# Half blocks with their two parts stacked, one more group of x copied out of PSUM, and three low halves of the weights made by GpSimd

## The chip, the cores and the metric

The kernel runs on one core of a Trainium2 chip. The metric is the device time of one execution in microseconds. Before the change it is 1144.92 us, the median of three runs (1144.85 to 1145.62).

## What is computed

Attention over channels, and behind it a layer of eight experts of which each token takes one:

```python
qn = q / (norm(q, axis=1) + 1e-6);  kn = k / (norm(k, axis=1) + 1e-6)   # B=4, N=5056, C=256
s = kn.transpose(0, 2, 1) @ qn / tau                                    # 256 x 256 a batch
a = softmax(s, -1)
x = (v @ a).reshape(20224, 256)
logits = x @ w_gate                                                     # 8 experts
e = argmax(logits);  gate_w = softmax(logits)[e]
out = gate_w * (relu(x @ w1[e]) @ w2[e])                                # w1 256 x 1024, w2 1024 x 256
```

## The kernel before

**Two float16 parts for each number.** A float32 number is held as a high and a low float16 part, and a product is three matmuls: high by high, high by low, low by high. The weights are sixteen half matrices (w1 and w2 of eight experts, 128 x 4096 float16 each with both parts, in the tile W). For each, `w_high` (ScalarE, L147) writes the high parts and `w_low` (VectorE, L151) the low ones, from float32 data that were loaded into the place of a neighbouring half matrix. So the halves are made in two chains, one from each end: the odd half of a pair may be written only when the low part of the even half has been read out, and the next pair begins behind that. In `lay`'s names they are ("high", i, k) and ("low", i, k), with even i in one chain and odd i in the other.

**The opening, up to about 140 us.** SyncE loads batch 0 of q and k (raw), the weights (W, wraw), batch 1 of q and k, and v. TensorE multiplies what has come: the products q·k (px, then sp, L187), a sum of squares of each weight half for its scale (gram, L128), and x of batch 0. x goes by groups g of 512 tokens in T = 4 tiles of 128 (`product`, L1205, 4 banks of PSUM, the tile px4; one more column by `bound`, L1210). The first AHEAD = 8 groups are read where they stand in px4: VectorE chooses the experts (`chosen`, L392 to L402) and a scale (`scaled`, L93), ScalarE writes the rows' high parts (L368), VectorE the low ones (L372), `rank` on TensorE (L421, L424) and `slots` give each token its place, and GpSimd scatters the four tiles' rows to DRAM (L460, DMA_INDIRECT). Groups 8 and 9 of batch 0 and all of batches 1 to 3 go by another way: one tile in a PSUM buffer of the pool ps_a, copied out by ScalarE (`copied`, L1299), and then worked on from SBUF (xg, two buffers). The pseudo task "handed" closes px4 and opens the PSUM pools of the expert blocks; the first block's first product waits for all reads of px4.

**The blocks.** A block is a run of sorted tokens of one expert: 72 blocks of 256 tokens while the batches come in, then 13 of 128 and 5 of 64 (half blocks). It needs eight pieces of weights, 128 x 1024 float16 each, copied from W to wp by VectorE (L734) or ScalarE (L741), because the expert's number is known only on the chip. `first` (L752) makes h = w1·x, with 12 matmuls a piece; `relu` (ScalarE, L760) and `rest` (VectorE, L763) write h's two parts to ht; `second` (L776) makes y with the token tile as weights (128 x 128, and 128 x 64 in a half block) and 256 columns of w2, six matmuls a piece and tile of tokens; `result` (ScalarE, L790) scales y and `store` (GpSimd, L794) scatters it to the output.

**What sets the order.** The programs of TensorE, ScalarE, VectorE and SyncE are written out by `lay`, a list planner: each `task` has an engine, a cost in us, the tasks it needs, a due time, and rings of buffers. Costs and due times decide only the order; on the chip each engine runs its own list in order and waits for semaphores. Pieces may go to ScalarE if it is free earlier. GpSimd's transfers are spaced by the planner's `RUN` and `REST`.

## Time and profile before

| | |
|---|---|
| median of three runs | 1144.92 us |
| the profiled execution | 1141.65 us, of which 1139.6 us are the span |
| TensorE (PE) busy | 1123.1 us, 99% of the span |
| VectorE (DVE) | 883.9 us, 78% |
| ScalarE (ACT) | 751.7 us, 66% |
| GpSimd (POOL) | 352.2 us, 31% |
| chain that ended last | TensorE 86%, DMA 7%, issue 3%, VectorE 2% |

A row of the timeline gives the start in us, the length, the engine, the line, the operation and its tiles, the number of equal instructions in the row, and, in brackets, for how long the engine stood idle and what ended that. TensorE's matmuls overlap: the distance from one row's start to the next row's start is what the row costs, and its length is longer than that.

### The profile page before, as it was taken

How to read it: one execution, taken by the hardware profiler on the slowest of the kernel's cores; microseconds unless marked ns; L12 is line 12 of the kernel's file. 1: busy time of each engine (PE TensorE's matmuls, PEld its weight loads, DVE VectorE, ACT ScalarE, POOL GpSimd, SP SyncE). 2: the span in 40 equal slices, each digit the busy share in tenths (PEclk: the TensorE clock that was granted, in tenths of full speed). 3: DMA queues.
4: the chain of work that ended last, by engine and by line, in shares of the span. 5: the costliest groups of instructions: out<-in, count | busy, mean ns of one | idle time of the engine just before them, and what ended most of it. 6: DMA issues, size and time to landing. Idle time of an engine off the chain costs nothing.

```text
span 1139.6 us, 28806 instructions
## 1 busy us (share of the span) xinstructions
PE 1123.1 (99%) x10325; PEld 985.8 (87%) x10325; DVE 883.9 (78%) x2562; ACT 751.7 (66%) x1558; POOL 352.2 (31%) x335
## 2 busy tenths in 40 slices
PE   9889999999999999999999999999999999999997
PEld 8778788988888878888888877888888888888897
DVE  6798686888888867778788876778777777867886
ACT  5565587698887877679897787477766555332232
POOL 0035442245334401243434411224343323232121
PEclk9999999999999999999999999999999999999999
DMA  9999688267764665265765575333332223222221
GB/s 367 408 406 354 168 266 261 71 183 211 198 205 115 168 186 143 76 176 146 202 205 146 127 211 171 75 93 96 104 103 66 75 57 73 57 76 53 46 43 40
DMA packets 155859, 177.42 MB, mean 156 GB/s; under 512 B 116866, under 2 KB 117124, under 8 KB 155712
## 3 DMA queue, kind: packets, MB, share of 16 engines
q1 hardware_dynamic: 139968, 132.74, 42.0%
q0 software_dynamic: 15744, 42.79, 11.1%
q8 instruction: 83, 1.36, 0.5%
q14 instruction: 64, 0.52, 0.1%
HBM read 111.48 MB, written 42.97 MB: 136 GB/s over the span
## 4 chain that ended last, share of the span: by engine, by line
PE 86%; DMA 7%; issue 3%; DVE 2%; POOL 1%; ACT 0%; SPq 0%; POOLq 0%; ACTq 0%
PE y L776 35%; PE hp L752 34%; PE px L1293 7%; DMA raw<-in_qk 4%; PE sp L209 3%; DMA W<-in_w 3%; PE sp L187 2%; PE px L1205 2%; PE sp L210 2%; POOL out L794 1%; DMA v<-in_vT 1%; PE px L1286 1%; PE px L187 0%; DVE ht L763 0%; DVE rows L372 0%
## 5 line engine op out<-in xcount | busy, mean ns | idle before, releaser
L776 PE MATMUL y<-wp,ht 128*128 128x256 f16 (+1 forms) x3888 | 482.2, 273 | 0.0
L752 PE MATMUL hp<-xT,wp 128*128 128x256 f16 (+2 forms) x4320 | 476.7, 260 | 0.5 <-DVE wp L734 0.5
L752 PEld LDWEIGHTS <-wp 128*128 128x128 f16 x4320 | 383.0, 98 | 46.7 <-DVE wp L734 3.2
L776 PEld LDWEIGHTS <-ht 128*128 128x128 f16 (+1 forms) x3888 | 376.1, 98 | 45.6 <-DVE ht L763 0.2
L734 DVE COPY wp<-W 128x1024 f16 x637 | 274.4, 443 | 112.5 <-PE hp L752 84.5
L760 ACT ACTIVATE ht<-hp 128x512 f16<-128x512 f32 (+1 forms) x324 | 189.7, 587 | 198.3 <-PE hp L752 180.9
L794 POOL DMA_INDIRECT out<-o,mt x162 | 168.2, 1038 | 480.2 <-ACT o L790 365.0
L460 POOL DMA_INDIRECT xs<-rows,r_si x160 | 178.5, 1116 | 294.9 <-ACT W L147 70.5
L763 DVE SCALAR_TENSOR_TENSOR ht<-hp,ht 128x512 f16<-128x512 f32 (+1 forms) x324 | 219.1, 677 | 33.9 <-ACT ht L760 32.1
L790 ACT ACTIVATE o<-y,b_fac 128x256 f32<-128x256 f32 (+1 forms) x162 | 69.2, 468 | 53.4 <-PE y L776 35.0
L1293 PE MATMUL px<-a_h,hl 128*128 128x264 f16 x480 | 99.4, 276 | 0.0
L741 ACT COPY wp<-W 128x1024 f16 x83 | 85.6, 1040 | 3.5 <-PE y L776 2.6
L1293 PEld LDWEIGHTS <-hl 128*128 128x128 f16 x720 | 68.5, 98 | 9.5
L179 DVE SCALAR_TENSOR_TENSOR hl<-raw,qk_s,hl 128x512 f16<-128x512 f32 x80 | 56.5, 747 | 23.0 <-ACT hl L172 23.0
L172 ACT ACTIVATE hl<-raw,qk_s 128x512 f16<-128x512 f32 x80 | 53.3, 713 | 21.8 <-PE sp L210 20.7
L1293 PE MATMUL px<-a_l,hl 128*128 128x264 f16 x240 | 66.2, 276 | 0.0
L1425 ACT ACTIVATE nraw<-nraw 128x1024 f32<-128x1024 f32 x60 | 63.1, 1052 | 2.1 <-DMA nraw<-in_qkc 2.1
L1299 ACT COPY xg<-px 128x264 f32<-128x264 f32 x128 | 47.4, 371 | 24.7 <-PE px L1293 19.1
L368 ACT ACTIVATE rows<-xg,x_sc 128x256 f16<-128x256 f32 x128 | 55.9, 500 | 9.2 <-DVE x_sc L93 8.8
L1305 ACT ACTIVATE xjunk<-xg 128x256 bf16<-128x256 f32 x128 | 53.1, 415 | 2.8
L372 DVE SCALAR_TENSOR_TENSOR rows<-xg,x_sc,rows 128x256 f16<-128x256 f32 x128 | 54.8, 476 | 0.0
L209 PE MATMUL sp<-hl 128*128 128x512 f16 x160 | 54.2, 379 | 0.0
(227 smaller groups left out, 956.8 us busy)
## 6 DMA issues: line engine op xcount, KB each, us to landing
raw<-in_qk SPq DMA_DIRECT2D x80, 512.0 KB, 4.6
nraw<-in_qkc SPq DMA_DIRECT2D x60, 512.0 KB, 4.5
vraw<-in_vT SPq DMA_DIRECT2D x32, 512.0 KB, 3.9
W<-in_w SPq DMA_DIRECT2D x28, 512.0 KB, 10.2
v<-in_vT SPq DMA_DIRECT2D x16, 256.0 KB, 9.2
out<-o,mt POOLq DMA_INDIRECT x162, 3.6
xs<-rows,r_si POOLq DMA_INDIRECT x160, 3.9
wraw<-in_w SPq DMA_DIRECT2D x4, 512.0 KB, 9.6
```

What stands on the lines that cost most here:

```text
L209: pe.matmul(sp[c], hl[:, 0, j, kc0 : kc0 + P], hl[:, :, j, 0:C], start=first, stop=False)
L460: ins = pool.indirect_dma_start(out=xs[:, :], out_offset=bass.IndirectOffsetOnAxis(ap=si[:n, t : t + 1], axis=0), in_=rows[:n, t, :], in_o ...
L734: mark[0] = vec.tensor_copy(out=wps[n], in_=Wf[:, ds(b["e"] * 8192 + n * 1024, 1024)])
L741: mark[0] = act.copy(out=wps[n], in_=Wf[:, ds(b["a"] * 8192 + n * 1024, 1024)])
L752: mark[0] = pe.matmul(hps[f // nf][:, f % nf, :], wp[:, dc, wh, (f % 2) * P : (f % 2 + 1) * P], xT[:, 2 * xh + dc, 0:nt], start=(n == 0), ...
L760: mark[0] = act.activation(hts[h][:, 0], hps[h], AF.Relu)
L763: mark[0] = vec.scalar_tensor_tensor(out=hts[h][:, 1], in0=hps.pop(h), scalar=0.0, in1=hts[h][:, 0], op0=ALU.max, op1=ALU.subtract)
L776: mark[0] = pe.matmul(ys[j], hts[f // nf][:, hh, f % nf, j * tall : (j + 1) * tall], wp[:, f % 2, wh, :], start=(f == 0 and j == 0 and n = ...
L790: act.activation(b["o", j][0:tall], ys[j], AF.Copy, scale=b["fac"][0:tall, j : j + 1])
L794: pool.indirect_dma_start(out=out[:, :], out_offset=bass.IndirectOffsetOnAxis(ap=load()[1].bitcast(I32)[0:tall, j, 1:2], axis=0), in_=b.po ...
L1293: pe.matmul(pt, hl[:, vh, c, ts], ah[:, c, :], start=(n == 0), stop=(n == 5))
L1425: act.activation(raw, raw, AF.Square, accum_out=sums[b][:, n // 5, n % 5 : n % 5 + 1])
```

## The change

Five edits.

1. **Stacked halves.** In a half block ht is laid out so that the high and the low part of 64 tokens lie side by side, 128 columns in all, and are loaded as one 128 x 128 set of weights. `second` then multiplies them with w2's high and with its low part: two matmuls in place of three. Partitions 0 to 63 of y hold what the high part gives, 64 to 127 what the low part gives. `result` scales the lower half into o, and a new VectorE step, `whole`, adds the scaled upper half. `factor` becomes two instructions, one for each half of the partitions.
2. **The order of the last blocks.** Before, the half blocks stand between the first of the 128-token blocks, one behind each; now they are spread over all 13.
3. **The eighth group (g = 7) of x** is copied from px4 to xg by ScalarE (`taken_out`, APART = 7), tile by tile, and its rows, choice and so on read xg. "handed" then waits for these copies and for `scaled`, no longer for the group's `high`, `low` and `chosen`.
4. **Three low halves on GpSimd.** For ("low", 2, 0), ("low", 4, 0) and ("low", 6, 0) VectorE's one instruction becomes two of GpSimd: the float32 data times the scale, in place, and the difference to the high parts. The planner reserves 7.0 us for the two, against 2.35 for VectorE's one.
5. **Costs in the plan**: a piece 0.38 (0.45), `vsc` 0.5 (0.25), `chosen` 1.0 (0.9), `count` 0.67 (0.6), `weighed` 0.76 (0.52) for batches 1 to 3.

```diff
+APART = 7
+ON_POOL = ((2, 0), (4, 0), (6, 0))
...
     def w_low(i, k):
         d4, src, sw = w_parts(i, k)
+        if (i, k) in ON_POOL:
+            pool.tensor_scalar(out=src, in0=src, scalar1=sw, scalar2=None, op0=ALU.mult)
+            pool.tensor_tensor(out=d4[:, :, 1, :], in0=src, in1=d4[:, :, 0, :], op=ALU.subtract)
+            return
...
         def relu(h):
-            hts[h] = work.tile([P, 2, nf, nt], F16, tag="ht", name="ht", bufs=4)
+            if stacked:
+                hts[h] = work.tile([P, nf, 2, nt], F16, tag="ht", name="ht", bufs=4).rearrange("p f s n -> p s f n")
+            else:
+                hts[h] = work.tile([P, 2, nf, nt], F16, tag="ht", name="ht", bufs=4)
...
             for f in (2 * k, 2 * k + 1):
-                for j in range(nj):
+                for wh in range(2) if stacked else ():
+                    mark[0] = pe.matmul(
+                        ys[0], hts[f // nf][:, :, f % nf, :], wp[:, f % 2, wh, :],
+                        start=(f == 0 and wh == 0), stop=(f == 7 and wh == 1),
+                    )
+                for j in range(0 if stacked else nj):
...
-            act.activation(b["o", j][0:tall], ys[j], AF.Copy, scale=b["fac"][0:tall, j : j + 1])
+            act.activation(b["o", j][0:tall], ys[j][P - tall : P], AF.Copy, scale=b["fac"][P - tall : P, j : j + 1])
+
+        def whole():
+            vec.scalar_tensor_tensor(
+                out=b["o", 0][0:tall], in0=ys[0][0:tall], scalar=b["fac"][0:tall, 0:1], in1=b["o", 0][0:tall],
+                op0=ALU.mult, op1=ALU.add,
+            )
...
-            task(("low", i, k), vec, 2.35, [("high", i, k)], call(w_low, i, k), 6)
+            task(("low", i, k), *((pool, 7.0) if (i, k) in ON_POOL else (vec, 2.35)), [("high", i, k)], call(w_low, i, k), 6)
...
-    stages += [one for two in zip(bigs, smalls) for one in two] + bigs[SMALL:]
+    for k in range(BIG):
+        stages += [bigs[k]] + smalls[(k * SMALL + BIG - 1) // BIG : ((k + 1) * SMALL + BIG - 1) // BIG]
...
+    def taken_out(g, t):
+        if t == 0:
+            at["xg", 0, g] = work.tile([P, T, C + E], F32, tag="xg", name="xg", bufs=2)
+        bank(t, act.copy(out=at["xg", 0, g][:, t, :], in_=px[:, t, 0 : C + E]))
...
+            if g >= APART:
+                for t in range(T):
+                    task(("cp", 0, g, t), act, 0.33, [("x", 0, g, t)] + ([("cp", 0, g, t - 1)] if t else []), call(taken_out, g, t), 2,
+                         takes=[("xg", 2)] if t == 0 else [], uses=[("xg", 0)])
+                made = [("cp", 0, g, T - 1)]
...
-    task("handed", None, 0.0, [(what, 0, g, t) for g in range(AHEAD) for t in range(T) for what in ("high", "low")]
-         + [("chosen", 0, g) for g in range(AHEAD)] + [("most", i) for i in range(E)], handed, 0)
+    task("handed", None, 0.0, [(what, 0, g, t) for g in range(min(AHEAD, APART)) for t in range(T) for what in ("high", "low")]
+         + [("chosen", 0, g) for g in range(min(AHEAD, APART))]
+         + [what for g in range(APART, AHEAD) for what in [("scaled", 0, g)] + [("cp", 0, g, t) for t in range(T)]] + [("most", i) for i in range(E)], handed, 0)
...
-            task(("piece", n, k), vec, 0.45, [("expert", n)], lambda by, k=k: piece(k, by), d(2 * k + 1) - 2, takes=[("wp", WP)])
+            task(("piece", n, k), vec, 0.38, [("expert", n)], lambda by, k=k: piece(k, by), d(2 * k + 1) - 2, takes=[("wp", WP)])
...
-            task(("second", n, k), pe, 1.32 if nj == 2 else 0.66, [("piece", n, 4 + k), ("rest", n, h)] + ([("second", n, k - 1)] if k else []),
+            task(("second", n, k), pe, 1.32 if nj == 2 else 0.44 if stacked else 0.66, [("piece", n, 4 + k), ("rest", n, h)] + ([("second", n, k - 1)] if k else []),
...
+            if stacked:
+                task(("whole", n), vec, 0.4, [("result", n, j)], whole, d(15) + 4, uses=[("o", 0), ("y", 0), ("b_fac", 0)])
```

**Where the order moves: the weights in the opening.** GpSimd's list begins with the scatters of x's first groups (rows are the data, r_si the places); W is the tile of weights. Before:

```order
L460 DMA xs_78<-rows_693,r_si_738 164096x258 x4
L460 DMA xs_78<-rows_834,r_si_880 164096x258 x4
L460 DMA xs_78<-rows_972,r_si_1004 164096x258 x4
L460 DMA xs_78<-rows_1074,r_si_1099 164096x258 x4
L460 DMA xs_78<-rows_1165,r_si_1189 164096x258 x4
```

After:

```order
L154 TENSOR_SCALAR W_79<-W_79,scales_80 128x2048
L155 TENSOR_TENSOR W_79<-W_79 128x8x256
L466 DMA xs_78<-rows_683,r_si_718 164096x258 x4
L154 TENSOR_SCALAR W_79<-W_79,scales_80 128x2048
L155 TENSOR_TENSOR W_79<-W_79 128x8x256
L466 DMA xs_78<-rows_820,r_si_867 164096x258 x4
L466 DMA xs_78<-rows_931,r_si_966 164096x258 x4
L154 TENSOR_SCALAR W_79<-W_79,scales_80 128x2048
L155 TENSOR_TENSOR W_79<-W_79 128x8x256
L466 DMA xs_78<-rows_1058,r_si_1099 164096x258 x4
```

The three pairs of new instructions stand ahead of the scatters of groups 0, 1 and 3. ScalarE's list at the same time, where each W row is a `w_high` that may wait for a low part (vsq are v's squares for `bound`, r_d and rows belong to a group of x). Before:

```order
L147 ACTIVATE W_79<-W_79,scales_80 128x8x256 x6
L1200 ACTIVATE vsq0_669<-v0_325 128x512
L1200 ACTIVATE vsq1_684<-v1_326 128x512
L147 ACTIVATE W_79<-W_79,scales_80 128x8x256
L1226 ACTIVATE r_d_677<-r_d_677 128x32
L368 ACTIVATE rows_693<-px4_81,x_sc_691 128x256 x4
L443 ACTIVATE rows_693<-kt_125 128x4
L147 ACTIVATE W_79<-W_79,scales_80 128x8x256 x2
```

After:

```order
L149 ACTIVATE W_79<-W_79,scales_80 128x8x256 x6
L1250 ACTIVATE r_d_639<-r_d_639 128x32
L374 ACTIVATE rows_683<-px4_81,x_sc_681 128x256 x4
L449 ACTIVATE rows_683<-kt_125 128x4
L1224 ACTIVATE vsq0_705<-v0_325 128x512
L1224 ACTIVATE vsq1_711<-v1_326 128x512
L149 ACTIVATE W_79<-W_79,scales_80 128x8x256 x2
L1224 ACTIVATE vsq0_790<-v0_359 128x512
L1224 ACTIVATE vsq1_792<-v1_360 128x512
L149 ACTIVATE W_79<-W_79,scales_80 128x8x256
```

The first group's rows now come ahead of the seventh and eighth `w_high`, and the squares of the third group of v stand behind them.

**The hand-over to the blocks, ScalarE.** px_81 or px4_81 is the PSUM of the first eight groups, xg a group in SBUF, the other px one tile of group 8, hp a block's product. Before:

```order
L1425 ACTIVATE nraw,n_sums<-nraw 128x1024
L1226 ACTIVATE r_d<-r_d 128x32
L368 ACTIVATE rows<-px_81,x_sc 128x256 x4
L443 ACTIVATE rows<-kt 128x4
L1299 COPY xg<-px 128x264
L1305 ACTIVATE xjunk,x_ss<-xg 128x256
L1299 COPY xg<-px 128x264
L1305 ACTIVATE xjunk,x_ss<-xg 128x256
L760 ACTIVATE ht<-hp 128x512 x2
```

After:

```order
L1328 COPY xg_1412<-px4_81 128x264 x4
L374 ACTIVATE rows_1460<-xg_1412,x_sc_1458 128x256 x4
L449 ACTIVATE rows_1460<-kt_125 128x4
L1250 ACTIVATE r_d_1463<-r_d_1463 128x32
L1323 COPY xg_1498<-px_1455 128x264
L1334 ACTIVATE xjunk_1518,x_ss_1517<-xg_1498 128x256
L770 ACTIVATE ht_1531<-hp_1500 128x512
```

The four copies come first and the rows are made from the copy; the first `relu` stands behind one tile of group 8 and not behind three.

**The last blocks, ScalarE.** A 128x512 ht is half a block of 128 tokens, 128x256 or 128x4x64 half a half block, and a 64x256 o a half block's result. Before:

```order
L760 ACTIVATE ht<-hp 128x512
L790 ACTIVATE o<-y,b_fac 64x256
L760 ACTIVATE ht<-hp 128x512
L760 ACTIVATE ht<-hp 128x256
L790 ACTIVATE o<-y,b_fac 128x256
L760 ACTIVATE ht<-hp 128x256
L760 ACTIVATE ht<-hp 128x512
L790 ACTIVATE o<-y,b_fac 64x256
```

After:

```order
L807 ACTIVATE o<-y,b_fac 64x256
L770 ACTIVATE ht<-hp 128x512 x2
L807 ACTIVATE o<-y,b_fac 128x256
L770 ACTIVATE ht<-hp 128x512 x2
L807 ACTIVATE o<-y,b_fac 128x256
L770 ACTIVATE ht<-hp 128x512
L770 ACTIVATE ht<-hp 128x4x64
L807 ACTIVATE o<-y,b_fac 128x256
L770 ACTIVATE ht<-hp 128x4x64
L770 ACTIVATE ht<-hp 128x512
L807 ACTIVATE o<-y,b_fac 64x256
```

Between two half blocks there were one block of 128 tokens before, and now two or three.

## Rows read from the trace of the kernel before

**Rows 1.** The page: TensorE's share, and the chain that ended last.

```profile
PE 1123.1 (99%) x10325; PEld 985.8 (87%) x10325; DVE 883.9 (78%) x2562; ACT 751.7 (66%) x1558; POOL 352.2 (31%) x335
PE 86%; DMA 7%; issue 3%; DVE 2%; POOL 1%; ACT 0%; SPq 0%; POOLq 0%; ACTq 0%
```

**Rows 2.** Waits of TensorE: for what, us in total, times, longest.

```profile
PE gram L128 <- DMA W<-in_w: 2.5, 3, 1.4
PE sp L187 <- DMA raw<-in_qk: 2.1, 2, 1.6
PE px L1286 <- ACT xg L1299: 2.1, 1, 2.1
...
PE hp L752 <- DVE wp L734: 0.5, 1, 0.5
```

**Rows 3.** Windows: length, busy us of PE, PEld, DVE, ACT, POOL, clock, DMA.

```profile
60.00:80.00 20.00, 18.51 (x178) 16.28 (x177) 19.25 (x38) 15.37 (x20) 6.26 (x4) 1.00 1.03 405
...
100.00:120.00 20.00, 20.00 (x121) 17.10 (x120) 12.52 (x38) 7.94 (x19) 10.50 (x10) 1.00 0.81 278
...
1060.00:1080.00 20.00, 20.00 (x291) 17.62 (x288) 16.83 (x45) 5.59 (x12) 3.78 (x4) 1.00 0.26 42
...
1100.00:1120.00 20.00, 20.00 (x276) 18.98 (x274) 17.44 (x43) 5.73 (x12) 3.96 (x4) 1.00 0.23 55
```

**Rows 4.** Timeline of TensorE: one half block among blocks of 128 tokens.

```profile
1070.17 0.84 PE L752 MATMUL hp<-xT,wp 128*128 128x128 f16 x12
1070.94 0.84 PE L776 MATMUL y<-wp,ht 128*64 128x256 f16 x6
1071.72 0.84 PE L752 MATMUL hp<-xT,wp 128*128 128x128 f16 x12
...
1074.61 0.51 PE L752 MATMUL hp<-xT,wp 128*128 128x64 f16 x12
1074.95 0.82 PE L776 MATMUL y<-wp,ht 128*128 128x256 f16 x6
...
1077.62 1.18 PE L752 MATMUL hp<-xT,wp 128*128 128x64 f16 x24
1078.73 1.50 PE L776 MATMUL y<-wp,ht 128*64 128x256 f16 x12
1080.16 0.84 PE L752 MATMUL hp<-xT,wp 128*128 128x128 f16 x12
```

**Rows 5.** The same view, where only blocks of 128 tokens are left.

```profile
1105.19 0.83 PE L752 MATMUL hp<-xT,wp 128*128 128x128 f16 x12
1105.86 0.82 PE L776 MATMUL y<-wp,ht 128*128 128x256 f16 x6
1106.51 0.83 PE L752 MATMUL hp<-xT,wp 128*128 128x128 f16 x12
```

**Rows 6.** Timeline of the hand-over to the blocks: TensorE, VectorE, ScalarE.

```profile
135.76 1.14 PE L1286 MATMUL px<-a_x,vraw 128*128 128x264 f32 x4
135.94 0.19 DVE L392 TENSOR_REDUCE r_m<-px 128x4 f32<-128x32 f32 x1 [2.76 <-PE px L1210]
...
137.08 0.19 PE L421 MATMUL rtp<-r_ex,tri 128*128 128x32 f16 x1 [0.19 <-DVE r_ex L402]
...
138.97 0.40 ACT L1299 COPY xg<-px 128x264 f32<-128x264 f32 x1
139.42 1.16 PE L1286 MATMUL px<-a_x,vraw 128*128 128x264 f32 x4 [2.06 <-ACT xg L1299]
```

**Rows 7.** Line L151, VectorE's low halves: ns least/median/most, first and last start.

```profile
L151 DVE SCALAR_TENSOR_TENSOR W<-W,scales x14: 2340/2342/2351, 49.9 to 98.1; 128x2048 f16<-128x2048 f32 x14
```

**Rows 8.** Timeline of GpSimd's scatters, and VectorE's low halves beside them.

```profile
77.30 0.96 POOL L460 DMA_INDIRECT xs<-rows,r_si  x1 [0.30 <-DVE scales L93]
...
83.18 4.61 DVE L151 SCALAR_TENSOR_TENSOR W<-W,scales 128x2048 f16<-128x2048 f32 x2
83.60 2.75 POOL L460 DMA_INDIRECT xs<-rows,r_si  x1 [0.30 <-DVE rows L372]
```

More of the change, by code (lines that the diff above doesn't have):

```diff
@@ L721, in block @@
         nf = min(4, 512 // nt)
+        stacked = nt < P
         wps, hps, hts, ys = {}, {}, {}, []
@@ L799, in store @@
             )
-        return nj, nf, expert, piece, first, relu, rest, second, factor, result, store
+        return nj, nf, expert, piece, first, relu, rest, second, factor, result, whole, store
     px = ps_x.tile([P, T, 512], F32, name="px4")
@@ L1236, in high @@
         ins = row_high(at["rows", b, g], x(), at["sc", b, g], t)
-        if ("ss", b, g) not in at:
+        if b == 0 and g < min(AHEAD, APART):
             bank(t, ins)
@@ L1241, in low @@
         ins = row_low(at["rows", b, g], x(), at["sc", b, g], t)
-        if ("ss", b, g) not in at:
+        if b == 0 and g < min(AHEAD, APART):
             bank(t, ins)
@@ L1356, in group @@
             made, summed_ = [("cp", b, g, T - 1)], [("xsq", b, g, T - 1)]
+        apart = not four or g >= APART
         task(("scaled", b, g), vec, 0.12, summed_, call(scaled, b, g), end, takes=[("rows", 3), ("x_sc", 2)],
@@ L1505, in block_tasks @@
         loads = {}
-        nj, nf, expert, piece, first, relu, rest, second, factor, result, store = block(
+        nj, nf, expert, piece, first, relu, rest, second, factor, result, whole, store = block(
             st, lambda: tables[st], i, lambda: loads[0]
@@ L1513, in block_tasks @@
         d = lambda eighth: block_due(n, eighth)
-        whole = (1.32, 0.67, 0.35)[max(0, st - LAST + 1)]
+        products = (1.32, 0.67, 0.35)[max(0, st - LAST + 1)]
+        stacked = SIZE[st] < P
         tab = done_with(st)
@@ L1567, in attention_then_experts @@
             load = block_load(LAST, tables[LAST], i)
-            nj, nf, expert, piece, first, relu, rest, second, factor, result, store = block(
+            nj, nf, expert, piece, first, relu, rest, second, factor, result, whole, store = block(
                 LAST, lambda: tables[LAST], i, lambda: load
```

37 lines of the change are left out of this document (20 added, 17 removed).

## The prediction

> **What bounds the kernel now.** I read the page's busy shares and its chain first, then who TensorE waits for, then windows, and last the timeline at the places that the change touches. TensorE is busy for 1123.1 of 1139.6 us and makes 86% of the chain [rows 1]. So the time is TensorE's work plus its few waits, and each edit is worth what it takes from the one or the other. The waits are short and nearly all in the first 140 us: 2.5 us for weights, 2.1 for chunks of q and k, 2.1 for ScalarE's copy of a tile of group 8 [rows 2]. Behind that there is almost nothing to win from VectorE or ScalarE: the blocks' wait for pieces is 0.5 us in all [rows 2].
>
> The opening has two halves. From 60 to 80 us the DMA engines are full (share 1.03, 405 GB/s), VectorE is busy for 19.25 of 20 us, and TensorE for 18.51; from 100 to 120 us TensorE is busy all the time and the DMA share is 0.81 [rows 3]. TensorE first waits for loads, and then has a backlog that it works off without a break. Time that it loses before 100 us is made good only as far as a wait for a load would have stood there anyway.
>
> The sum is made against the profiled execution: 1141.65 us, a span of 1139.6 and 2.05 around it. The median of the runs is 1144.92, 3.27 above it; I carry the difference over to the median.
>
> **Stacked halves, fewer matmuls.** A half block's `second` has 8 steps of three matmuls; two of three stay. That is 8 matmuls less in each of five half blocks, 40 in all. Six of them with a 128 x 128 tile take 1074.95 to 1075.61, 0.66 us or 0.110 each [rows 4]. 40 x 0.110 = **-4.4 us**, all on TensorE's path.
>
> **Stacked halves, no narrow tiles.** Six `second` matmuls with 64 columns of weights take longer than six with 128: 1070.94 to 1071.72 is 0.78 us against 0.66, and the twelve `first` ahead of them take 0.77 (1070.17 to 1070.94) against 0.67 in the stretch with blocks of 128 tokens alone (1105.19 to 1105.86) [rows 4, 5]. So each run of narrow matmuls costs 0.11 + 0.12 us, at its beginning and in it. The run of twelve shows the same: 1078.73 to 1080.16 is 1.43 us where 12 x 0.110 make 1.32, and the row before it takes 1.11 where 12 x 0.029 (0.34 us for the twelve of 64 columns, 1074.61 to 1074.95) and 0.67 make 1.01 [rows 4, 5]. Three runs a half block are 3 x 0.22 = 0.65 us, five half blocks **-3.3 us**. The stacked form loads 128 columns throughout, so I count all of it as gone; the bounds are 0 and -3.3.
>
> **The new order of the last blocks, and VectorE.** What hid VectorE's work was the half block's slow `second`. One block of 128 tokens and one half block take 9.99 us (1070.17 to 1080.16) [rows 4] and need 16.83 x 9.99/20 = 8.4 us of VectorE [rows 3]. A block of 128 alone takes 4 x 1.32 = 5.28 us (1105.19 to 1106.51, four times) [rows 5] and 17.44 x 5.28/20 = 4.6 us of VectorE [rows 3]. So a half block costs VectorE 3.8 us. The change adds a second `factor` and `whole`, for which no row stands: as bounds I take 0.38 us (two of the smallest 0.19 us rows) and 0.95 (the low halves' 2.34 for 2048 columns scaled to 512, 0.58, and 0.38 beside it) [rows 6, 7], and use 0.65 as their middle. Afterwards a half block takes TensorE 4 x 0.34 + 16 x 0.110 = 3.1 us and VectorE 4.45: VectorE falls behind by 1.3 at each. Each block of 128 gives 0.7 back, and there are two or three between half blocks, 1.4 to 2.1. In the old order of one to one, the faster half block would be bound by VectorE; in the new one it just fits, and five buffers of pieces bridge the rest. I take **+0.4 us**, bounds 0 and 2.5.
>
> **The hand-over.** Now `rank` of the eighth group waits 0.19 us, and the second tile of group 8 waits 2.06 us for a copy that stands behind four `high` rows on ScalarE [rows 2, 6]. After the change that copy has a matmul run of a block between itself and the next tile, and the block's first product needs only the copies and `scaled`. What is late next is `rank` itself. VectorE's choice takes from 135.94 to 137.08 until `rank` begins, 1.14 us [rows 6], and can now start only when the last copy is made, about 0.40 us (one copy) later [rows 6]. `rank` would stand about 1.5 us behind the start of the next tile, where before it came at 137.08 - 135.76 = 1.3; but only one tile of group 8 is multiplied ahead of it, half of what stood there, so TensorE waits about 1.2 us. From 2.25 us of waits 1.2 stay, with a little for latencies: **-1.0 us**, bounds 0 and -2.2.
>
> **Three low halves on GpSimd.** VectorE loses 3 x 2.34 = 7.0 us of work [rows 7]. That buys little by itself: TensorE waits for loads in this stretch, not for VectorE. The cost is in what waits. ScalarE's `w_high` of the other half waits for GpSimd's second instruction, and behind it on ScalarE stand v's squares, the exponentials and the high rows of the next groups of x; without those TensorE gets no `bound` and no next group, as px4 is read out late. Behind the new instructions on GpSimd itself stand the scatters of groups 0, 1 and 3, and the rows' three buffers are held until they have gone.
>
> The plan allows 7.0 us a pair. No row shows GpSimd doing arithmetic. From below, it takes no less than twice VectorE's 2.34, 4.7 us [rows 7]. From above: a scatter takes 0.96 us alone and 2.75 beside two of VectorE's low halves, 2.9 times as long [rows 8], and 2.9 x 4.7 = 13.5. The nearest to the plan's number with company is 7.0 plus one such lengthening, 2.75 - 0.96 = 1.8, so about 9 us. The three pairs are in one chain (each even pair of halves waits for the one before), so 2 us too long each make ScalarE some 6 us late at the end of it. TensorE takes up part of that: it waited 2.5 us for weights and about as much again for chunks in the opening [rows 2], and a late TensorE finds its loads there. 6 - 4 = **+2.0 us**, bounds -3.5 (the load waits shrink because the order is better, and GpSimd disturbs nothing) and +9.5 (13.5 us a pair, half of the 19.5 us taken up by the backlog).
>
> A scatter beside VectorE's low half takes nearly three times as long [rows 8]. The Trainium skill (SBUF — State Buffer, "SBUF: two separate sides") calls the ports that VectorE and GpSimd share an exclusive lock: an instruction of VectorE with two inputs in SBUF and one of GpSimd that reads SBUF exclude each other for their whole length. By that VectorE's low halves, and its small steps of the choice with two inputs in SBUF, would stand still too, while rows 7 show none that ran longer than 2.351 us, with nothing longer than a scatter beside it. By that page the sum would be that of the second rival below.
>
> **Costs in the plan.** They move rows everywhere, but TensorE's waits behind 140 us are so few (0.5 us for pieces [rows 2]) that the new order can hardly win; it can lose. I take **+0.3 us**, bounds -0.5 and +3.
>
> **Sum.** -4.4 - 3.3 + 0.4 - 1.0 + 2.0 + 0.3 = -6.0 us, a span of 1133.6 and a median of **1138.9 us**.
>
> **Rivals.**
>
> *The opening gets better too.* For it: VectorE is relieved by 7 us where it is busiest (19.25 of 20 us [rows 3]), and x's second group now comes one half of a weight's sum earlier. Against it: the loads set the pace there. The opening's term is then -3.5 to 0 in place of +2.0: -11.5 to -8 us, 1133.4 to 1136.9.
>
> *GpSimd and VectorE lock each other out.* For it: the stretched scatter [rows 8]. Each pair meets at least one of VectorE's low halves and a choice; if VectorE stands behind GpSimd's second instruction, `rank` of group 0, now right behind a weight's sum on TensorE, stops TensorE, and so on twice more. Three times 2.34 to 4 us, less 1 to 2 that the load waits take up, are +5 to +10; with 6.0 + 2.0 = 8.0 us of gain elsewhere that leaves -3 to +2. Its middle, +6.5, gives 1143.4. Against it: VectorE needs the lock in only a part of its rows, and the plan's 7.0 may contain it.
>
> *Slower: GpSimd takes 12 us or more a pair.* In the chain of three each us above 7 counts three times on ScalarE. With 4 us taken up, 3 x (T - 7) - 4 = 8 is reached at T = 11: from there the change loses. At T = 12.5 it is +12.5, 1149.4 us. For it: 2.9 times, as the scatters show, would be 13.5. Against it: ScalarE stood idle for several us between its rows there (busy for 15.37 of 20 us [rows 3]), so not all of the lateness reaches TensorE.
>
> *The narrow tiles' 0.22 us stays,* because it belongs to the change between the blocks' two kinds of products. Then -2.7: 1142.2. Against it: blocks of 128 tokens change as often and don't show it [rows 5].
>
> **How the numbers follow.** The forecast, 1137 to 1141, gets 0.52; the better opening 0.22; the lock 0.15; slower GpSimd 0.06; the narrow tiles 0.05. For 8 in 10 the range takes in nearly all of the better opening and the near half of the lock: 1134 to 1143. What a measurement can tell from no change is about 0.2%, 2.3 us. Faster than 1142.6 are the forecast, the better opening, most of the narrow tiles and near half of the lock: 0.86. Within 0.2%: a good third of the lock and a bit of the others, 0.08. Slower: 0.06, the slow GpSimd and the far end of the lock.
>
> **What would show it.** In the profile after: 40 fewer `second` matmuls, and 1.1 us from one run of four to the next with no row of 0.77 us in the last 90 us; TensorE's wait for xg at the hand-over gone and one for VectorE's choice in its place; GpSimd's TENSOR_SCALAR and TENSOR_TENSOR near 9 us together, with ScalarE's W rows waiting for them; VectorE's low halves still 2.34 us. I am wrong if TensorE waits for VectorE's pieces among the last blocks for more than 2.5 us, if it waits in the opening for choices or ScalarE's rows by more than the loads' waits shrink, or if new waits of a us stand in the blocks between 140 and 1040 us.

## The result and the profile after

The changed kernel takes 1155.56 us (median of six runs, 1152.73 to 1158.75) where the kernel before takes 1144.65 (1142.69 to 1145.62) beside it: a ratio of 1.0099, interval 1.0085 to 1.0113. It is slower by 11 us where 6 us of gain were forecast. The profiled execution took 1152.73 us, its span is 1151.0, which is 11.4 us more than the span of the profile of before.

The page of after, TensorE's share and the chain, beside [rows 1]:

```profile
PE 1122.3 (98%) x10285; PEld 985.2 (86%) x10285; DVE 887.0 (77%) x2571; ACT 749.0 (65%) x1560; POOL 381.9 (33%) x341
PE 83%; DVE 6%; DMA 6%; ACT 2%; issue 1%; another core or an unknown queue 0%; POOL 0%; SPq 0%; DVEq 0%; ACTq 0%; POOLq 0%
```

The 40 matmuls are gone (10285 for 10325), but VectorE's part of the chain has risen from 2% to 6%. The waits of TensorE, beside [rows 2]:

```profile
PE px L1229 <- DVE rows L378: 6.7, 4, 2.6
PE wtp L137 <- DVE w_dsum L134: 5.6, 3, 4.7
PE y L791 <- ACT wp L748: 2.6, 1, 2.6
PE rtp L427 <- DVE r_ex L408: 1.4, 1, 1.4
...
PE sp L193 <- DMA raw<-in_qk: 1.0, 1, 1.0
```

The waits for weights (2.5 us) and half of those for chunks are gone, and the wait for xg at the hand-over too. In their place TensorE waits for VectorE, at three of its products: x's next group waits for the low rows of the group before it, a weight's total for its maxima, a `rank` for a choice. That is 6.7 + 5.6 + 1.4 = 13.7 us of waits for VectorE in the opening, where the trace of before has 0.7 (0.5 for a total, 0.2 for a `rank`). The windows, beside [rows 3] (the last two are shorter ones):

```profile
60.00:80.00 20.00, 16.39 (x142) 14.41 (x141) 18.71 (x29) 11.64 (x15) 16.90 (x6) 1.00 1.03 406
100.00:120.00 20.00, 16.28 (x71) 13.28 (x71) 14.13 (x19) 7.29 (x11) 13.31 (x4) 0.83 0.48 166
85.00:90.00 5.00, 4.72 (x14) 3.78 (x15) 4.00 (x8) 2.00 (x1) 4.92 (x2) 0.66 1.04 399
105.00:110.00 5.00, 5.00 (x20) 3.78 (x20) 2.78 (x3) 2.00 (x1) 3.65 (x2) 0.58 0.14 53
```

TensorE is busy for 16.39 us where it was busy for 18.51, and for 16.28 of 20 us where it never stood. Its granted clock, 1.00 throughout in [rows 3], falls to 0.66 and 0.58 (stretches at 1.2 GHz in place of 2.4) where it resumes after waits of 2.6 and 4.7 us. The sixteen matmuls of one group of x show what that costs; first TensorE's timeline in e10 (below: no pairs, full clock), then in after:

```profile
96.58 3.72 PE L1229 MATMUL px<-a_x,v 128*128 128x264 f32 x16
```

```profile
85.28 5.49 PE L1229 MATMUL px<-a_x,v 128*128 128x264 f32 x16 [2.60 <-DVE rows L378]
...
103.30 6.70 PE L1229 MATMUL px<-a_x,v 128*128 128x264 f32 x16
```

That is 1.8 + 3.0 = 4.8 us more.

What held VectorE is seen when GpSimd's pairs and VectorE's instructions of the same time are laid side by side. GpSimd's timeline (its scatters left out), then rows of VectorE's with what stands between them left out (start, length):

```profile
60.55 6.56 POOL L154 TENSOR_SCALAR W<-W,scales 128x2048 f32<-128x2048 f32 x1 [59.97 <-DMA W<-in_w]
67.19 5.20 POOL L155 TENSOR_TENSOR W<-W 128x2048 f16<-128x2048 f32 x1
...
80.89 5.46 POOL L154 TENSOR_SCALAR W<-W,scales 128x2048 f32<-128x2048 f32 x1
86.43 4.06 POOL L155 TENSOR_TENSOR W<-W 128x2048 f16<-128x2048 f32 x1
...
107.63 5.46 POOL L154 TENSOR_SCALAR W<-W,scales 128x2048 f32<-128x2048 f32 x1 [1.35 <-ACT W L149]
113.18 4.07 POOL L155 TENSOR_TENSOR W<-W 128x2048 f16<-128x2048 f32 x1
```

```profile
63.18 2.24 DVE L402 SCALAR_TENSOR_TENSOR r_eq<-r_d,kt 128x32 f32<-128x32 f32 x1
...
66.11 2.34 DVE L157 SCALAR_TENSOR_TENSOR W<-W,scales 128x2048 f16<-128x2048 f32 x1
...
68.70 0.18 DVE L455 TENSOR_TENSOR r_sl<-rtp,r_ex 128x32 f32<-128x32 f32 x1
...
69.23 3.17 DVE L439 SCALAR_TENSOR_TENSOR r_z<-r_z,x_sc 128x4 f32<-128x4 f32 x1
...
79.11 0.19 DVE L402 SCALAR_TENSOR_TENSOR r_eq<-r_d,kt 128x32 f32<-128x32 f32 x1
...
81.16 3.48 DVE L439 SCALAR_TENSOR_TENSOR r_z<-r_z,x_sc 128x4 f32<-128x4 f32 x1
...
87.75 4.89 DVE L157 SCALAR_TENSOR_TENSOR W<-W,scales 128x2048 f16<-128x2048 f32 x1 [0.97 <-ACT W L149]
...
110.67 0.73 DVE L402 SCALAR_TENSOR_TENSOR r_eq<-r_d,kt 128x32 f32<-128x32 f32 x1
...
113.27 6.12 DVE L157 SCALAR_TENSOR_TENSOR W<-W,scales 128x2048 f16<-128x2048 f32 x1 [0.77 <-ACT W L149]
...
119.84 0.16 DVE L439 SCALAR_TENSOR_TENSOR r_z<-r_z,x_sc 128x4 f32<-128x4 f32 x1
```

An instruction on four columns (r_z) takes 3.17 us where it takes 0.16 with no pair beside it, and ends at 72.40, as GpSimd's TENSOR_TENSOR does (67.19 + 5.20 = 72.39). The low half of 87.75 ends at 92.64, which is 2.34 after 90.30, when GpSimd's instruction was about to end (90.49). The other way round, GpSimd's TENSOR_TENSOR of 67.19 takes 5.20 in place of 4.06 and lies beside VectorE's low half that ends at 68.45, 1.26 later. What passes is `r_sl` (68.70, 0.18 us): its first input, rtp, lies in PSUM. In this trace, then, a VectorE instruction with two inputs in SBUF doesn't run together with either instruction of a pair (the first reads a tensor and its scales, the second two tensors; the last 1.7 us of the first don't count, see below), and the one that began first keeps the other waiting. The six held instructions take 20.63 us where they take 0.19 + 0.16 + 0.16 + 2.34 + 0.19 + 2.34 = 5.38: VectorE stood for 15.25 us, and had given away three low halves, 7.0 us.

### The profile page after: what moved, and what is told of

Same layout as the page of the kernel before. It is cut to its first block, busy times and chain, and to the rows that moved or that the text cites. A ratio compares the mean times of both kernels' runs of the same rounds, so it can differ in the third digit from the quotient of the medians.

```text
span 1151.0 us, 28740 instructions
## 1 busy us (share of the span) xinstructions
PE 1122.3 (98%) x10285; PEld 985.2 (86%) x10285; DVE 887.0 (77%) x2571; ACT 749.0 (65%) x1560; POOL 381.9 (33%) x341
## 4 chain that ended last, share of the span: by engine, by line
PE 83%; DVE 6%; DMA 6%; ACT 2%; issue 1%; another core or an unknown queue 0%; POOL 0%; SPq 0%; DVEq 0%; ACTq 0%; POOLq 0%
PE hp L759 34%; PE y L791 33%; PE px L1317 6%; DMA W<-in_w 4%; PE sp L215 3%; DVE W L157 2%; PE px L1229 2%; PE sp L216 2%; DMA v<-in_vT 1%; PE sp L193 1%; PE y L784 1%; PE px L1310 1%; DVE rows L378 1%; DMA raw<-in_qk 1%; DVE wp L741 1%
## 5 line engine op out<-in xcount | busy, mean ns | idle before, releaser
L791 PE MATMUL y<-wp,ht 128*128 128x256 f16 x3768 | 465.8, 273 | 2.8 <-ACT wp L748 2.6
L791 PEld LDWEIGHTS <-ht 128*128 128x128 f16 x3768 | 364.5, 98 | 47.7 <-issue 3.5
L741 DVE COPY wp<-W 128x1024 f16 x639 | 269.6, 437 | 108.5 <-PE hp L759 76.9
L748 ACT COPY wp<-W 128x1024 f16 x81 | 83.4, 1040 | 2.3 <-PE y L791 1.8
```

Of the source, the lines that this page charges most:

```text
L741: mark[0] = vec.tensor_copy(out=wps[n], in_=Wf[:, ds(b["e"] * 8192 + n * 1024, 1024)])
L748: mark[0] = act.copy(out=wps[n], in_=Wf[:, ds(b["a"] * 8192 + n * 1024, 1024)])
L791: mark[0] = pe.matmul(ys[j], hts[f // nf][:, hh, f % nf, j * tall : (j + 1) * tall], wp[:, f % 2, wh, :], start=(f == 0 and j == 0 and n = ...
```

## The experiments

The runs behind the first result came in five groups, each beside runs of the kernel before: e1 to e4 (before 1145.86), b2, e5, e6, e7 (1141.92), e8, e9, a2, e10 (1144.42), e12, e13, e14, b3 (1144.84), e15, e16 (1144.94). Before ran faster beside the second group than beside the others, so kernels are compared by their ratios to it, and differences are taken within a group where there is a choice.

**e1, no pairs on GpSimd; e2, the pairs alone in the kernel before.** For e1:

```diff
-ON_POOL = ((2, 0), (4, 0), (6, 0))
+ON_POOL = ()
```

> The changed kernel with all sixteen low halves on VectorE, everything else kept. Theory (lock): in the trace after, VectorE's instructions with two inputs in SBUF end only when GpSimd's instruction ends (r_z 3.17 us in place of 0.2, low halves 4.89 and 6.12 in place of 2.34), and the three pairs cost all of the loss. Then this is the forecast without its +2.0 for the pairs, 1136.9 us (1135 to 1139), every low half takes 2.34, no VectorE row is stretched, and the granted clock is 1.00 from 60 to 130 us. Rival (chain): the pairs cost the loss by their own length and what queues behind them; the same 1136.9 here, told apart by e3 and e4. Rival (the rest): the loss lies in the new plan costs or the hand-over; then 1144 us or more, with waits of several us left between 60 and 130.

e2 adds to the kernel before the lines of the change that make the pairs (in w_low and in the task of a low half), and no other.

> The kernel before with the three low halves on GpSimd alone (planned at 7.0), nothing else of the change. Lock and chain: the changed kernel's 1155.6 less the 1136.9 expected without the pairs is 18.7, so 1144.7 + 18.7 = 1163 us (1156 to 1168), with stretched VectorE rows and a granted clock under 1 between 80 and 120. Rival (the rest): 1143 to 1148. If the pairs do harm only together with the new costs in the plan, it is in between.

e1 took 1142.90 us, ratio 0.9979 (0.9968 to 0.9990); e2 1158.97, ratio 1.0119 (1.0104 to 1.0134). The pairs cost 1.0099 (from the first result) - 0.9979 = 12.0 per mille, 13.7 us, on top of the rest of the change, and 11.9 per mille, 13.6 us, without it: the loss is theirs. In e1's trace no low half is over 2.352 us. e2's waits are those of after (6.9 us for rows, 5.7 for maxima). But e1 gains 2.4 us where 8.0 were expected, so something else was off too.

**e3, e8, e9: three attempts that can't be read.** Pairs that nobody needs (e3, e8), or a wait of ScalarE for GpSimd of the same length (e9), were put on spare buffers, beside sixteen low halves on VectorE. e3 stands on e1, e8 and e9 on the stacked halves alone (e5, below). The lines of e8 and e9 that plan the work:

```diff
+        if i in SPARE:
+            task(("spare", i), pool, 7.0, [("high", i, 0)], call(w_spare, i), 1)
```

> e1 (all low halves on VectorE) plus the same two GpSimd instructions of 128x2048 at the second, fourth and fifth matrix, on places of W that are still empty (the multiplication is a minimum, the subtraction reads the true high half); nobody uses what they make. Lock: the work on VectorE is longer by 7.0 us than in the changed kernel and still stands behind each pair, 3.5 to 7 us a pair, of which the loads take up 1 to 2: e1 + 8 to e1 + 17, with r_eq, r_z or low halves that end together with a GpSimd instruction. Chain: nobody waits for the pairs but the scatters behind them: e1 + 0 to e1 + 1.5, VectorE's rows as long as in e1.

> e5 (stacked halves alone) plus pairs of the same kind on GpSimd at matrices 2, 4 and 6 that nobody waits for: two TENSOR_SCALAR of 128x1024 and one TENSOR_TENSOR of 128x2048 that reads the true high half, in buffers that are free then. VectorE's, ScalarE's and TensorE's orders are those of e5 to the row, and VectorE still makes all sixteen low halves. Lock: VectorE's rows with two SBUF inputs that meet a pair end with GpSimd's instruction (0.2 becomes 2 to 4, 2.34 becomes 4 to 6), and since VectorE is busy for 19 of 20 us there the time is 4 to 12 us over e5's. Chain: without anybody who waits for them the pairs cost 0 to 1.5 us, by the scatters behind them.

> e5 plus the wait without the pairs: at matrices 2, 4 and 6 GpSimd runs ten MEMSET of 128x1056 (a memset of 128x2048 took 1.80 us in e3, so 9.3 us together, as long as an undisturbed pair) between two tiny copies, and ScalarE's next high half waits for the last copy as it waits for a pair in the changed kernel; VectorE makes all low halves, and all other orders are e5's. Lock: a memset has no SBUF input, VectorE is not held, and only ScalarE's lateness is left: 1 to 5 us over e5. Chain: ScalarE's wait is what costs, 9 to 14 us over e5.

They gave 1172.91 (one of four runs 1669.66), 1169.18 and 1177.06 us (1.0237, 1.0214, 1.0288). The spare buffers were not spare: raw weights and chunks are loaded into the same memory in this stretch (in e3 the pairs even fell on raw weights that were there). In e8 the issuing queue stood for GpSimd:

```profile
SPq L1012 <- POOL spare L156: 43.6, 3, 21.7
```

SyncE's queue waited 16.5 us for GpSimd in e9 too, and in e3 TensorE 19.2 us for a pair. So these runs mix late loads into what they were to measure. e12 and e13 repeat e8 and e9 in memory that no load uses there.

**e4, the pairs in quarters.**

```diff
-            pool.tensor_scalar(out=src, in0=src, scalar1=sw, scalar2=None, op0=ALU.mult)
-            pool.tensor_tensor(out=d4[:, :, 1, :], in0=src, in1=d4[:, :, 0, :], op=ALU.subtract)
+            for q in range(0, 8, 2):
+                part = src[:, q : q + 2]
+                pool.tensor_scalar(out=part, in0=part, scalar1=sw, scalar2=None, op0=ALU.mult)
+                pool.tensor_tensor(out=d4[:, q : q + 2, 1, :], in0=part, in1=d4[:, q : q + 2, 0, :], op=ALU.subtract)
```

> The changed kernel with each of the three low halves made in four quarters (TENSOR_SCALAR and TENSOR_TENSOR of 128x512, eight instructions in place of two). Lock: VectorE gets in between them; a small row stands at most 1.4 us (a quarter of 5.46) in place of 3.5, and half or more of the 18.7 us goes: 1141 to 1147. Chain: a pair takes as long as before, 9.5 us or a bit more, and so does what waits for it: 1154 to 1160.

1158.07 us, ratio 1.0103 (1.0083 to 1.0122): no better than whole pairs. The lock's number missed and the chain's hit, but not in the way that either meant. VectorE's low halves (first line), GpSimd's quarters (second and third: ns least, median, most), and who waited for GpSimd:

```profile
L159 DVE SCALAR_TENSOR_TENSOR W<-W,scales x11: 2342/2344/2872, 49.9 to 106.3; 128x2048 f16<-128x2048 f32 x11
L156 POOL TENSOR_SCALAR W<-W,scales x12: 1552/1562/3642, 60.3 to 117.7; 128x512 f32<-128x512 f32 x12
L157 POOL TENSOR_TENSOR W<-W x12: 1141/1156/3199, 64.5 to 120.3; 128x512 f16<-128x512 f32 x12
...
ACT W L149 <- POOL W L157: 20.7, 3, 10.2
```

VectorE is held for half a microsecond at most. Now GpSimd stands behind VectorE's whole low halves: a quarter takes up to 3.64 in place of 1.55 us, the three low halves end 14.8, 12.7 and 14.5 us after they began, and ScalarE waits 20.7 us for them where it waited 1.6 in after. Cutting the instructions in four only changed who loses.

**e5 and e14, the stacked halves alone** (the same kernel in two groups): of the change only the stacked form and the new order of the last blocks.

```diff
-ON_POOL = ((2, 0), (4, 0), (6, 0))
+ON_POOL = ()
-APART = 7
+APART = 8
-            task(("piece", n, k), vec, 0.38, [("expert", n)], lambda by, k=k: piece(k, by), d(2 * k + 1) - 2, takes=[("wp", WP)])
+            task(("piece", n, k), vec, 0.45, [("expert", n)], lambda by, k=k: piece(k, by), d(2 * k + 1) - 2, takes=[("wp", WP)])
...
```

> The kernel before with the stacked halves and the new order of the last blocks alone: on every engine its instructions stand as before up to about 1045 us. By the forecast's steps -4.4 - 3.3 + 0.4 = -7.3 us, 1138.6 from 1145.9 (1137.5 to 1140). Theory (costs): so it is, and e1's missing 5.6 us are the new costs' or the hand-over's. Rival (stacked is worth less): the 0.22 us a run of narrow tiles stays or VectorE binds the last blocks, 1141 to 1143.

> e5 (stacked halves alone) once more, beside the others: 0.9935 of before if the chip has no part in it, and 0.996 to 0.998 if e1's and e10's smaller gain (0.9979, 0.9964) was the chip's and not the hand-over's.

1134.07 us, ratio 0.9935 (0.9923 to 0.9947), and 1137.59 us, 0.9938 (0.9924 to 0.9951): -7.4 and -7.1 us by their ratios, against the forecast's -7.3. This version beats both kernels.

**e6 and e7, new costs or copies taken back** from e1; **b2**, the kernel before again.

```diff
-        task(("count", b, g), vec, 0.67 if b else 0.2, [("chosen", b, g)], call(count, b, g), rk - 1, takes=[("r_ex", 3)])
+        task(("count", b, g), vec, 0.6 if b else 0.2, [("chosen", b, g)], call(count, b, g), rk - 1, takes=[("r_ex", 3)])
...
```

e6 puts back the five costs that differ; e7 sets APART to 8 and keeps them.

> The kernel before, unchanged, for a second trace of it. The profile of before ran 1141.65 us while its median is some 3 to 4 us more, and e1 (no pairs on GpSimd) gained 3.0 us where 8.0 were forecast. Theory (costs): that gap lies in e1 itself; then this trace has TensorE's waits behind 140 us as the first one had them (0.5 us for pieces, 0.7 for xg), and a span of 1139 to 1141. Rival (typical run): the first trace was a lucky execution, and this one has waits of 1 us or more at places between 160 and 400 us that the first doesn't show, and a span of 1142 to 1144.

> e1 (no pairs on GpSimd) with the plan's costs for pieces, choices, counts, weights and v's scale as in the kernel before: the stacked halves and the eighth group's copies remain. Theory (costs): -7.3 and -1.0 for the hand-over, 1137.6 us (1136 to 1139), some 5 us under e1, and the 2.6 us wait for a weight's piece at 170 us that e1 shows is gone. Rival (stacked is worth less): as e1, 1141 to 1143.

> e1 with the eighth group of x left in its four banks (new costs and stacked halves remain): the hand-over by itself. By the forecast's step +1.0 us on e1, 1143.9 (1142.9 to 1145), with the 2.1 us wait for xg back and none of 1.6 us for the choice at the hand-over. If the copies of the eighth group are what upset the order behind 160 us, it is 1139 to 1141 and the waits there are gone.

b2 ran 1143.02 us, its span 1141.0; TensorE's waits are those of the first trace. e6: 1135.35 us, 0.9943 (0.9930 to 0.9956). e7: 1134.10 us, 0.9937 (0.9924 to 0.9950). So in this group neither the costs (e7 against e5, +0.2 per mille) nor the copies (e6 against e5, +0.8, 0.9 us) cost the 5.6 us that e1 lacked, and e7's own two expectations were both missed. e6 has no wait at 170 us, as its theory wanted, but one of 2.4 us for a piece at 273 us. What was left was the group itself.

**a2, e10, e16, b3: the same kernels in other groups.** a2 is the changed kernel, e10 is e1, e16 is e7, b3 is before, none with an edit.

> The changed kernel once more, beside the others on one chip, for a second trace: 1.0099 of before. In the first trace TensorE stood from 98.2 to 102.8 us for a maximum whose matrix products were done at 96.3, and the signal of those products came at 102.3. If this belongs to the kernel, it is there again at the same place; if it belonged to the chip of the first runs, it is gone and the time is some 4 us less.

> e1 (no pairs on GpSimd) once more, beside the others. In e1's trace TensorE waited 5.6 us between 160 and 200 us and 4.3 between 250 and 400, and e7 (the same without the eighth group's copies) was 0.9937 of before where e1 was 0.9979. If the eighth group's copies cost that (theory: hand-over), this is 0.998 again and the waits are there. If it was the chip of those runs, this is 0.993 to 0.995.

> e7 (stacked halves and new costs, the eighth group left in its banks) once more. Theory (hand-over): the copies cost 3 to 4 us, and this is 0.993 to 0.9945 on any chip. Rival (chip): on a chip on which before takes 1144 us or more, this is 0.996 to 0.998, as e1 and e10.

> The kernel before for its trace on this chip. If the waits of 2.6 to 3 us for a piece at 166 to 182 us, which e1, e10 and the changed kernel show, belong to the hand-over of the eighth group or the new costs, they are not here; if they belong to the chip, waits of that kind are here too.

a2: 1153.10 us, 1.0087 (1.0070 to 1.0103), with the same waits at the same places as the first trace of after; beside it e10: 1139.93 us, 0.9964 (0.9947 to 0.9982). The pairs cost 12.3 per mille, 14.1 us, in this group. e10 has the 2.8 us wait for a piece that its theory named, but lies between its two expectations. e16, the same kernel as e7: 1141.18 us, 0.9975 (0.9963 to 0.9987), 3.8 per mille more than e7, and so in its rival's range. TensorE's and VectorE's timelines of e16 and, last, VectorE's of e7 at the same step, the counts of a sort:

```profile
161.93 0.17 PE L526 MATMUL ctp<-r_ex,ones 128*128 128x8 f16 x1
161.96 1.47 PE L791 MATMUL y<-wp,ht 128*128 128x256 f16 x12
...
166.91 2.36 PE L791 MATMUL y<-wp,ht 128*128 128x256 f16 x12 [2.17 <-DVE c_p L519]
...
164.74 0.15 DVE L529 SCALAR_TENSOR_TENSOR c_ni<-ctp,kt 1x8 int32<-1x8 f32 x1 [2.10 <-PE hp L759]
```

```profile
163.65 0.14 DVE L529 SCALAR_TENSOR_TENSOR c_ni<-ctp,kt 1x8 int32<-1x8 f32 x1
```

In e16 VectorE goes on 2.6 us after the product that it needs is done (162.1), and the trace names a later product, hp, as what released it; TensorE runs dry behind it, and its next row is 2.36 us long where the same row at 161.96 took 1.47. In e7 VectorE goes on at once. So it does at this step in b3 and e14 too; there TensorE's longest waits behind 140 us are 0.8 and 1.3 us. In e1, e10 and after it waits 2.6 to 2.8 us for a weight's piece between 166 and 185 us, a copy of ScalarE that stands behind a `relu`, which itself waits for a product.

What sets the second group apart shows in ScalarE's idle time ahead of a `relu` that the trace marks as issue, that is, with nothing that ended it: there is none in the traces of before, b2, e5, e6 and e7, and 3.6 to 10.4 us in each of the others. It is not the chip alone: the record gives the second and the fourth group the same one. What the condition costs seems to depend on what the plan has put behind the late steps: 3.7 per mille between e14 and e16 (old and new costs, in two groups), nothing between e5 and e7.

**e12, pairs that nobody waits for; e13, the wait without pairs.** Both on the stacked halves alone (e14 beside them), with sixteen low halves on VectorE; every other engine's instructions stand in e14's order.

```diff
+    def w_spare(i):
+        s16 = work.tile([P, 8, 256], F16, tag="junk", name="spare", bufs=1)
+        d4, src, sw = w_parts(i, 0)
+        one8 = ones[:, 0:1].unsqueeze(2).to_broadcast([P, 8, 256])
+        pool.tensor_scalar(out=s16, in0=one8, scalar1=sw, scalar2=None, op0=ALU.min)
+        pool.tensor_tensor(out=s16, in0=one8, in1=d4[:, :, 0, :], op=ALU.subtract)
```

> e5 (stacked halves alone) plus pairs that nobody waits for, at matrices 2, 4 and 6: a TENSOR_SCALAR of 128x2048 and a TENSOR_TENSOR of 128x2048 whose second input is the true high half, into a buffer of 4 KB a partition that nothing else uses from 45 to 125 us (e8 had a buffer that loads use too). All other engines' orders, SyncE's too, are e5's to the row; VectorE makes all low halves. Lock: VectorE's rows with two SBUF inputs that meet a pair end with GpSimd's instruction, and the time is 4 to 12 us over e14's. Chain: 0 to 1.5 us over e14's.

```diff
+        pool.tensor_copy(out=s32[:, 0:8], in_=d4[:, :, 0, 0])
+        for r in range(18):
+            pool.memset(s32, 1.0)
+        pool.tensor_copy(out=s32[:, 0:8], in_=src[:, :, 0])
```

> e5 plus the wait without the pairs: at matrices 2, 4 and 6 GpSimd runs eighteen MEMSET of 128x512 between two tiny copies, some 9 to 10 us, and ScalarE's high half of the sibling matrix waits for the last copy, as it waits for a pair in the changed kernel; the buffer is one that no load uses in this stretch (e9's was). VectorE makes all low halves; the other engines' orders are e5's to the row. Lock: VectorE is not held, and ScalarE's lateness alone costs 1 to 5 us over e14. Chain: 9 to 14 us over e14.

e12: 1148.59 us, 1.0036 (1.0025 to 1.0047), 9.8 per mille or 11.2 us over e14. e13: 1161.23 us, 1.0154 (1.0133 to 1.0175), 21.6 per mille or 24.7 us over e14. Two rows of VectorE's timeline in e12 (a low half, and a step of the choice that takes 0.19 us undisturbed), the low halves in e13 (the line's group), and ScalarE's wait there:

```profile
63.68 5.61 DVE L165 SCALAR_TENSOR_TENSOR W<-W,scales 128x2048 f16<-128x2048 f32 x1
...
97.01 4.29 DVE L410 SCALAR_TENSOR_TENSOR r_eq<-r_d,kt 128x32 f32<-128x32 f32 x1
```

```profile
L166 DVE SCALAR_TENSOR_TENSOR W<-W,scales x14: 2340/2342/2352, 49.8 to 110.6; 128x2048 f16<-128x2048 f32 x14
...
ACT W L158 <- POOL spare L154: 32.7, 3, 14.4
```

The lock alone, with nobody who needs the pairs, costs 11.2 us: it is inside the lock's expectation and far from the chain's. It isn't the changed kernel's price to the us, since VectorE makes three low halves more here, 7.0 us. The wait alone costs 24.7, more than either expected, and there VectorE is not held: no low half is over 2.352 us beside GpSimd's memsets. So a wait for GpSimd is dear where the plan doesn't know of it. In the changed kernel the plan does: ScalarE waits 1.6 us for a pair there (3.5 in a2), against 32.7 here, so that price was not paid.

**e15, the old order of the last blocks** with the stacked form.

```diff
-    for k in range(BIG):
-        stages += [bigs[k]] + smalls[(k * SMALL + BIG - 1) // BIG : ((k + 1) * SMALL + BIG - 1) // BIG]
+    stages += [one for two in zip(bigs, smalls) for one in two] + bigs[SMALL:]
```

> e14 (stacked halves alone) with the last blocks in their old order, one half block after each of the first five blocks of 128 tokens. By the forecast's step VectorE falls behind by 1.3 us at each half block and gets back 0.7 at each block of 128, so with four pairs in a row and five buffers of pieces TensorE waits 0.5 to 3 us more than in e14: 0.9943 to 0.9965 of before. Rival (the order has no part): 0.993 to 0.994.

1138.35 us, 0.9945 (0.9932 to 0.9958), 0.7 per mille over e14: it is at the near end of the forecast's range and the intervals overlap. From 1040 to 1120 us TensorE is idle for 1.3 us in e15's trace and for 0.8 in e14's. Whether the new order is needed is not settled.

## Why the prediction was wrong, point by point

**Fewer matmuls and no narrow tiles: right.** The timeline of after at a half block, beside [rows 4]:

```profile
1082.30 0.83 PE L759 MATMUL hp<-xT,wp 128*128 128x128 f16 x12
1082.97 0.60 PE L784 MATMUL y<-wp,ht 128*128 128x256 f16 x4
1083.41 0.83 PE L759 MATMUL hp<-xT,wp 128*128 128x128 f16 x12
```

Four matmuls in 0.44 us and twelve `first` in 0.67: a run takes 1.11 us, no row of 0.77 or 0.78 is left, and e5 and e14 measure -7.4 and -7.1 for these steps and the order's +0.4 together, forecast -7.3. The rival of the narrow tiles that stay slow falls. VectorE, the order's step, is at the edge as forecast: it is busy for 18.78 of 20 us among the last blocks (17.44 in [rows 3]), and TensorE doesn't stand in these 20 us.

```profile
1100.00:1120.00 20.00, 20.00 (x297) 18.96 (x295) 18.78 (x52) 6.58 (x14) 4.60 (x5) 1.00 0.31 56
```

**The hand-over: mechanism right, gain not shown.** The wait for xg is gone and `rank` waits for the choice, which begins only with the last copy, as forecast (1.2 us; 0.97 and a little for latencies):

```profile
149.99 1.14 PE L1310 MATMUL px<-a_x,vraw 128*128 128x264 f32 x4
150.96 0.17 DVE L398 TENSOR_REDUCE r_m<-xg 128x4 f32<-128x32 f32 x1
...
152.09 0.19 PE L427 MATMUL rtp<-r_ex,tri 128*128 128x32 f16 x1 [0.97 <-PE px L1310]
```

In time it is +0.9 us (e6 against e5), and against e16 -1.3 (e10) or +0.5 (e1), which stood in other groups: about zero, where -1.0 was forecast with bounds of 0 and -2.2.

**Three low halves on GpSimd: the step that failed, +13.7 us for +2.0.** Its parts:

- The length of a pair was right: 5.46 + 4.06 = 9.5 us undisturbed, forecast about 9.
- The 4 us that loads would take up were about right: e10, without the pairs, waits 4.0 us for loads in the opening, after 1.0.
- The chain on ScalarE, which made the +2.0, did not run: ScalarE waits 1.6 us for a pair in after, not 6. It has its own dear case: 20.7 us of such waits in e4, where the plan allows 7.0 us for a pair that takes 12.7 to 14.8, and 32.7 in e13, where the plan knows of no wait.
- The lock was left out of the sum, and by itself it costs 11.2 us (e12). In after VectorE stood for 15.25 us and saved 7.0. TensorE's waits ahead of the hand-over are 13.7 us for VectorE and 1.0 for a chunk, against the 4.5 of e10 below: 10.2 us more. With 4.8 lost to the clock that is 15.0, against 13.7 and 14.1 measured. Waits of 2.25, 2.60, 1.52, 1.37 and 0.36 us, 8.1 in all, stand right behind held instructions; the longest, 4.7 us at 98 us, with the 3.0 us of clock behind it, comes with the pairs (after, a2, e2), but no row ties it to the lock (see the end of this section).

```profile
PE gram L130 <- DMA W<-in_w: 2.4, 3, 1.1
...
PE sp L193 <- DMA raw<-in_qk: 1.1, 2, 0.9
...
PE wtp L137 <- DVE w_dsum L134: 0.5, 1, 0.5
PE gram L130 <- DMA wraw<-in_w: 0.5, 1, 0.5
```

The argument that failed is the one against the lock: rows 7 show no low half over 2.351 us, "with nothing longer than a scatter beside it". That says what a scatter does; no row of before had a GpSimd instruction that reads SBUF tensors, so there was nothing in it against the lock. The rival named the mechanism, was given 0.15, and was itself too small (+5 to +10): it counted one hold a pair, behind GpSimd's second instruction, while both instructions of a pair held VectorE (3.32 us behind the first and 2.55 behind the second of the pair at 80.89), and it left the clock out.

The Trainium skill (SBUF — State Buffer, "SBUF: two separate sides") had said it: an exclusive lock between a VectorE instruction with two SBUF inputs and a GpSimd instruction that reads SBUF, kept by whichever starts first. The traces agree on this, the memsets that hold nobody (2.352 us at most, e13) and the PSUM input that passes (0.18 us) included. They differ on its "for the whole instruction", as far as GpSimd's recorded ends, which are rough, can be relied on: during a TENSOR_SCALAR VectorE went on 3.75 us after its start (84.64 - 80.89) and 3.77 (111.40 - 107.63), in each case 1.7 us ahead of its recorded end, while a TENSOR_TENSOR held to about its end.

**Costs in the plan: +4.2 for +0.3.** In the second group they cost 0.2 us (e7 against e5), and between e14 and e16, of the two last groups, 3.7 per mille, 4.2 us. That is a bit beyond the forecast's +3, but the intervals of the two leave about 2 us either way. In e16's trace the place is the wait for the sort's counts at 162 to 167 us: 2.2 us, and 1.7 more in the two rows behind it, which take 2.15 and 2.13 us to the next start where 1.31 stood before. A wait of the kind stood nowhere in the trace of before, which like the second group's has none of ScalarE's unexplained idle time. That the costs alone bring it about is not shown, as no group holds both kernels.

The parts by the later measurements are -7.1 + 13.7 + 4.2 + (-1.3 to +0.5) = 9.5 to 11.3 us; the change measured 11.3 and, in a2, 10.0. They are differences along one chain of kernels (before, e14, e16, e1 or e10, after), so that they add up is no further test. Of the rivals, slow GpSimd at 12.5 us a pair came nearest with 1149.4 us, and by luck: the pairs took 9.5 to 11.8, and ScalarE's lateness, which made its sum, was not what cost the time.

**What stays open.** The longest single wait of after, 4.7 us at 98 us, is not explained. The timelines of TensorE and VectorE:

```profile
95.32 1.08 PE L130 MATMUL gram<-wraw 128*128 128x128 bf16 x16
96.23 1.94 PE L193 MATMUL sp<-raw 128*128 128x256 f32 x8
102.85 0.59 PE L137 MATMUL wtp<-w_dsum,ones 128*128 128x2 f32 x2 [4.67 <-DVE w_dsum L134]
```

```profile
102.37 0.42 DVE L134 TENSOR_REDUCE w_dsum<-gram 128x2 f32<-128x256 f32 x1 [5.68 <-remote]
```

VectorE needs the sixteen products that were done at 96.4, is free from 96.7, and begins at 102.37; the trace shows no instruction of this core that released it. It is so in both traces of after and in e2, and not in b3, e1, e10 or e14; it may be of the same kind as the late step in e16. It is counted in the pairs' 13.7 us; e12, where every wait of TensorE that is over 3 us stands behind a held instruction, costs 11.2 without it.

## What to carry to other kernels

Work moved from VectorE to GpSimd is not taken off VectorE if the two read SBUF at the same time: look up which of VectorE's instructions have two SBUF inputs and which of GpSimd's read SBUF, and add to VectorE's side the time of GpSimd's that meets them, small instructions on the path to TensorE first. A trace that never shows the new instruction says nothing for or against what it will do beside the others; its absence is a reason to widen a bound, and no evidence. And price a short TensorE wait by what follows it too: two waits of 2.6 and 4.7 us cost another 4.8 at the lower clock.
